# Forward transform moved ahead of the loop, gradient through a padded scratch, last 64 rows of D row-tiled

## Chip, cores, metric

One core of one Trainium2 chip. The metric is device time of the whole program in microseconds (us). Times are medians, and runs of one kernel lie within 0.5%. Profile times count from the span's start; the span is some 2 to 4 us shorter than the device time.

## The reference

Forward and gradients of a gated mix of two branches: a spectral filter (a 2-D real Fourier transform, a product with weights, the inverse) and a GEGLU feed-forward block.

```python
# x, B_x: 1 x 2048 x 576; w_gate, w_up: 576 x 4608; w_down: 4608 x 576; bfloat16
g = sigmoid((x * gate_w).sum(-1))
a = irfft2(rfft2(x) * (w_r + 1j * w_i))
b = (gelu(x @ w_gate) * (x @ w_up)) @ w_down
out = g * a + (1 - g) * b
# plus the gradients of all inputs but B_x for a given grad_out (all weights and A_x)
# x of both branches is A_x
```

## The kernel before

Everything is written as matmuls. The long loop has 18 groups (256 of the 4608 hidden columns each) of 8 steps (256 rows each). A step does the *hidden matmuls* (gate, up, and gradient through w_down), their elementwise work on ACT and DVE, one or two *weight gradient units* of the group before, and some *transform units* (pieces of the Fourier work) out of a list. After the loop come the output projections.

D is 576 = 4 x 128 + 64. The last chunk was taken as rows 448 to 575, with its first 64 rows zeroed on one side:

```python
DCH = [(0, 128), (128, 128), (256, 128), (384, 128), (448, 128)]
...
def load_dOT(t0):                      # gradient, transposed, 32 small loads
    for t in (t0, t0 + 1):
        LD.dma_start_transpose(dOT[:, 0:4, t, :], do_v[:, t, 0:512])
        LD.dma_start_transpose(dOT[:, 4:5, t, :], do_v[:, t, DCH[4][0]:D])
    nc.gpsimd.memset(dOT[0:D4NEW, 4, t0:t0 + 2, :], 0.0)
...
ph = ...tile_pool(name="ph", bufs=4, space=PSUM)   # hidden matmuls, 1 bank each
pw = ...tile_pool(name="pw", bufs=2, space=PSUM)   # weight gradients
pf = ...tile_pool(name="pf", bufs=1, space=PSUM)   # transform units, 2 banks
...
def H_mm(g, tp):
    for w, xt in ((wg_g, xT), (wu_g, xT), (wdT_g, dOT)):
        pt = ph.tile([P, TPB, FG], F32, tag="hps", name="hps")
        for tt in range(TPB):
            for ci in range(5):
                nc.tensor.matmul(pt[:, tt, :], lhsT=xt[:, ci, tp * TPB + tt, :], rhs=w[:, ci, :],
                                 start=(ci == 0), stop=(ci == 4))
...
fft = fx[:4] + at + fx[4:] + fg + mid[:-2] + ...   # fx: x's transform, fg: the gradient's
def want(step, half):                  # how many units by this half step
    h = 2 * step + half
    if h <= 2 * NT:
        n = max(0, h - 4)              # 12 units in group 0
```

PSUM is the memory that matmuls write to, in banks. A transform unit is a few matmuls into `pf` in PSUM, a copy out by ACT (or DVE) to `Y` or `Vt`, and often a store (x's units store `Vt` to `scr_x`). `LD` is the sync engine's (SP's) DMA queue, which issues in program order.

## Time and profile before

| | before |
|---|---|
| device time | 1581.0 us |
| span | 1576.6 us |
| first hidden matmul | 9.5 us |
| group 0 | 73.0 us |
| groups 1 to 15 | 923.9 us, 61.6 each |
| group 16 (no transform units) | 50.0 us |
| first matmul of the output projections | 1130.2 us |

PE (the matrix engine) carries the time: it is at work 96% of the span, and half of its idle time (35 of 66.5 us) lies in the first 160 us. The lines are in the prediction below. Two habits help in reading them. The "mean ns" of a matmul is a latency; the spacing of starts is what a stream costs. And the busy share of a whole run says little about a stage, so the starts of the groups, read from the timeline, are what everything here is measured by.

### The profile page before, as it was taken

To read this page: it belongs to the slowest core of one execution; us is meant where nothing else is said; L and a number is where in the kernel's file an instruction comes from. 1 tells how busy PE (TensorE), PEld (TensorE's weight loads), DVE (VectorE), ACT (ScalarE), POOL (GpSimd) and SP (SyncE) were. 2 spreads that over 40 slices of the span, in tenths; PEclk is the share of its full clock that TensorE was granted. 3 is DMA by queue.
4 is the path that set the end of the run, shared out by engine and by line. 5 is a ranking of instruction groups with operands and counts; after the bars stand their busy time and mean duration, and the time that the engine had idled before them with its cause. 6 is when DMAs were issued, how large, how long until landed. Compare 5 with 4: busy or idle time off the path is not lost.

```text
span 1576.6 us, 33157 instructions
## 1 busy us (share of the span) xinstructions
PE 1510.1 (96%) x13310; PEld 1270.9 (81%) x13310; DVE 813.9 (52%) x2154; ACT 738.8 (47%) x1395; POOL 26.3 (2%) x58
## 2 busy tenths in 40 slices
PE   6798999999999999999999999999997999999998
PEld 4577888888788888888888888888876777777776
DVE  5775565666887877865555646667103212121210
ACT  6777665765766766665666656656000000000000
POOL 1000000000000000000000000000000000000000
PEclk8999999999999999999999999999999999999999
DMA  6632432334544544453424434364899978787873
GB/s 140 198 102 78 113 99 82 109 97 132 140 134 120 151 124 129 132 152 93 124 82 135 127 97 128 101 145 122 241 192 214 212 153 172 155 171 154 170 150 69
DMA packets 513435, 214.45 MB, mean 136 GB/s; under 512 B 318080, under 2 KB 506368, under 8 KB 513280
## 3 DMA queue, kind: packets, MB, share of 16 engines
q1 hardware_dynamic: 511648, 207.61, 54.5%
q0 software_dynamic: 1632, 4.72, 1.1%
q8 instruction: 104, 1.70, 0.5%
q14 instruction: 51, 0.42, 0.1%
HBM read 41.77 MB, written 94.71 MB: 87 GB/s over the span
## 4 chain that ended last, share of the span: by engine, by line
PE 62%; issue 23%; DVE 6%; ACT 6%; DMA 1%; POOL 1%; SPq 1%; POOLq 0%; DVEq 0%; ACTq 0%
PE hps L312 25%; PE wps L392 15%; PE wps L376 7%; PE pf L640 3%; PE acc L833 2%; PE wps L403 2%; PE pf L433 2%; PE acc L875 2%; ACT da L334 1%; ACT om L330 1%; ACT q L323 1%; DMA pin<-scr 1%; PE pf L624 1%; PE pf L626 1%; ACT xb L324 1%
## 5 line engine op out<-in xcount | busy, mean ns | idle before, releaser
L312 PEld LDWEIGHTS <-xT 128*128 128x128 bf16 x2880 | 286.0, 99 | 39.6
L875 PEld LDWEIGHTS <-pin 128*128 128x128 bf16 x2304 | 225.4, 98 | 58.3 <-DMA pin<-scr 1.6
L392 PEld LDWEIGHTS <-xn 128*128 128x128 bf16 x2304 | 223.9, 98 | 30.3 <-issue 3.6
L312 PE MATMUL hps<-wg_g,xT 128*128 128x256 bf16 x1440 | 186.5, 278 | 0.0
L312 PE MATMUL hps<-wu_g,xT 128*128 128x256 bf16 x1440 | 183.8, 275 | 0.0
L312 PE MATMUL hps<-wdT_g,dOT 128*128 128x256 bf16 x1440 | 180.8, 273 | 0.0
L325 DVE TENSOR_SCALAR s<-q 128x512 bf16<-128x512 bf16 x144 | 42.0, 291 | 254.0 <-ACT q L323 253.8
L312 PEld LDWEIGHTS <-dOT 128*128 128x128 bf16 x1440 | 141.0, 98 | 16.4
L833 PE MATMUL acc<-wd_all,pin 128*128 128x288 bf16 x1152 | 145.4, 288 | 8.1 <-DMA pin<-scr 6.6
L376 PE MATMUL wps<-dB,A 128*128 128x288 bf16 x1152 | 152.2, 286 | 0.0
L875 PE MATMUL acc<-wuT,pin 128*128 128x288 bf16 x1152 | 143.4, 286 | 1.3 <-DMA pin<-scr 1.3
L833 PEld LDWEIGHTS <-pin 128*128 128x128 bf16 x1152 | 113.2, 98 | 38.5 <-DMA pin<-scr 7.5
L875 PE MATMUL acc<-wgT,pin 128*128 128x288 bf16 x1152 | 143.4, 286 | 0.0
L376 PEld LDWEIGHTS <-A 128*128 128x128 bf16 x1152 | 112.7, 98 | 27.6
L392 PE MATMUL wps<-dHu,xn 128*128 128x256 bf16 x1152 | 131.7, 273 | 0.0
L392 PE MATMUL wps<-dHg,xn 128*128 128x256 bf16 x1152 | 131.5, 273 | 0.0
L323 ACT ACTIVATE q<-hps 128x512 bf16<-128x512 f32 x144 | 86.1, 598 | 94.9 <-PE hps L312 94.9
L885 ACT COPY f32t<-acc 128x576 f32<-128x576 f32 x16 | 10.2, 638 | 250.5 <-PE acc L875 250.5
L334 ACT ACTIVATE da<-hps,omg 128x256 bf16<-128x256 f32 x288 | 118.1, 460 | 0.0
L887 DVE SCALAR_TENSOR_TENSOR f32t<-gwf,dlog,f32t 128x576 f32<-128x576 f32 x16 | 13.1, 818 | 179.1 <-ACT f32t L885 179.1
L330 ACT ACTIVATE om<-s 128x512 bf16<-128x512 bf16 x144 | 91.0, 632 | 24.5 <-DVE s L326 23.9
L331 ACT ACTIVATE s<-s 128x512 bf16<-128x512 bf16 x144 | 90.7, 630 | 4.6
(164 smaller groups left out, 1760.9 us busy)
## 6 DMA issues: line engine op xcount, KB each, us to landing
scr<-A SPq DMA_DIRECT2D x144, 128.0 KB, 1.9
scr<-dHg SPq DMA_DIRECT2D x144, 128.0 KB, 1.9
scr<-dHu SPq DMA_DIRECT2D x144, 128.0 KB, 1.9
out_dram<-dw SPq DMA_DIRECT2D x72, 128.0 KB, 1.8
out_dram<-dwd SPq DMA_DIRECT2D x36, 144.0 KB, 2.0
wd_all<-in_B_w_down_dram SPq DMA_DIRECT2D x3, 1728.0 KB, 12.6
scr_p<-Vt SPq DMA_DIRECT2D x32, 144.5 KB, 2.3
Vp<-scr_p SPq DMA_DIRECT2D x16, 289.0 KB, 3.4
```

Of the source, the lines that this page charges most:

```text
L312: nc.tensor.matmul(pt[:, tt, :], lhsT=xt[:, ci, tp * TPB + tt, :], rhs=w[:, ci, :], start=(ci == 0), stop=(ci == 4))
L323: nc.scalar.activation(q[:], hg[:], ACT.Square)
L325: V.tensor_scalar(s[:], q[:], A_GELU, 1.0, op0=ALU.mult, op1=ALU.add)
L330: nc.scalar.activation(om[:], s[:], ACT.Sigmoid, scale=-2.0 * C_GELU)
L331: nc.scalar.activation(s[:], s[:], ACT.Sigmoid, scale=2.0 * C_GELU)
L334: nc.scalar.activation(da[:, tt, :], da_ps[:, tt, :], ACT.Copy, scale=omg32[:, t0 + tt:t0 + tt + 1])
L376: nc.tensor.matmul(wps[:, :288], lhsT=tl(0, t)[:, fch * P:(fch + 1) * P], rhs=dB[:, t, h * 288:(h + 1) * 288], start=(t == 0), stop=(t == ...
L392: nc.tensor.matmul(wps[:, cc, :], lhsT=xn[:, t, (c0 + cc) * P:(c0 + cc + 1) * P], rhs=tl(k, t), start=(t == 0), stop=(t == T - 1))
L403: nc.tensor.matmul(wps[r0:r0 + 64, 0, :], lhsT=xn[:, t, 512:576], rhs=tl(k, t), start=(t == 0), stop=(t == T - 1))
L640: nc.tensor.matmul(yps[:, h, :288], lhsT=Z[:, lc, c, :], rhs=tb.At[lc][:, c, h * 288:(h + 1) * 288], start=(n == 0), stop=(n == 5))
L833: nc.tensor.matmul(bps[:, h, :288], lhsT=At[:, r, :], rhs=wd_all[:, fc, h * 288:(h + 1) * 288], start=(fc == 0), stop=(fc == NFC - 1))
L875: nc.tensor.matmul(xps[:, h, :288], lhsT=src[:, r, :], rhs=wT[:, h * 288:(h + 1) * 288], start=(k == 1 and f0 + r == 0), stop=(k == 2 and ...
```

## The change

The intent: (1) give the last 64 rows of D to half of the array's rows, two row tiles at once, so that five matmuls become four and a half; (2) put gate and up side by side in one 512-column matmul; (3) run x's part of the first stage of the transform (all of its 32 units, up to the store to `scr_x`) before the loop, while weights and gradient load; (4) replace 32 small transposing loads of the gradient by a padded copy in DRAM and four large ones; (5) retune the pace of units and the order on ACT. Core of the diff, cut:

```diff
+    for k in range(4):
+        load_x(4 * k)
+    do_s = [dram.tile([4, P, 5 * P], BF16, name=f"do_s{k}") for k in range(4)]
+    for k in range(4):
+        src = do_v[:, 4 * k:4 * k + 4, :].rearrange("p t d -> t p d")
+        LD.dma_start(do_s[k][:, :, 0:D], src)
+        LD.dma_start(do_s[k][:, :, D:], src[:, :, 512:D])
     wts = {0: load_w(0)}
+    for k in range(4):
+        LD.dma_start_transpose(dOT[:, :, 4 * k:4 * k + 4, :].rearrange("d c t p -> d c (t p)"),
+                               do_s[k][:].rearrange("t p d -> (t p) d"))
...
-    ph = ps1.enter_context(tc.tile_pool(name="ph", bufs=4, space=PSUM))
+    ph = ps1.enter_context(tc.tile_pool(name="ph", bufs=1, space=PSUM))   # xy, 2 banks
+    pz = ps1.enter_context(tc.tile_pool(name="pz", bufs=1, space=PSUM))   # z, 2 banks
...
+        if tp % 2 == 0:                               # z for two steps
+            ... 16 full matmuls of 256 columns ...
+            for t in range(t0, t0 + 4):
+                r = (LO, HI)[t % 2]
+                nc.tensor.matmul(zt[0][:, t % 2, (t - t0) // 2, :], lhsT=dOT[r, 4, t, :], rhs=wdT[r, 4, :],
+                                 start=False, stop=t >= t0 + 2)
+        for tt, r in enumerate((LO, HI)):             # xy: gate and up
+            nc.tensor.matmul(xy[:, tt, :], lhsT=xT[r, 4, t0 + tt, :], rhs=wgu[r, 4, :], start=True, stop=False)
+        for tt in range(TPB):
+            for ci in range(4):
+                nc.tensor.matmul(xy[:, tt, :], lhsT=xT[:, ci, t0 + tt, :], rhs=wgu[:, ci, :], ...)
...
+    for t in range(T):                                # the head, before the loop
+        x1[t]()
+        ... transposes of x, tables ...
+        if t > 0:
+            x2[t - 1]()                               # ends in a store through LD
...
-            n = max(0, h - 4)
+            n = max(0, 3 * (h - 1) // 2)              # 22 units in group 0
```

More of the change, by code (lines that the diff above doesn't have):

```diff
@@ L37 @@
 IMM = bass.MemoryType
-def load_w_dchunks(nc, eng, dst, w, fsl):
-    eng.dma_start(dst[:, 0:4, :], w[0:512, fsl].rearrange("(c p) f -> p c f", p=P))
-    eng.dma_start(dst[:, 4, :], w[DCH[4][0]:D, fsl])
+LO, HI = slice(0, 64), slice(64, 128)
 class Unit:
@@ L66, in iotas @@
     G.iota(tb.dcol[:, 0:4], pattern=[[128, 4]], base=0, channel_multiplier=1, **kw)
-    G.iota(tb.dcol[:, 4:5], pattern=[[0, 1]], base=DCH[4][0], channel_multiplier=1, **kw)
+    for r in (LO, HI):
+        G.iota(tb.dcol[r, 4:5], pattern=[[0, 1]], base=512, channel_multiplier=1, **kw)
     tb.krow = res.tile([P, P], F32, name="krow")
@@ L211, in load_w @@
         fsl = slice(g * FG, (g + 1) * FG)
-        wg_g = wpool.tile([P, 5, FG], BF16, tag="wg_g", name="wg_g")
-        wu_g = wpool.tile([P, 5, FG], BF16, tag="wu_g", name="wu_g")
-        wdT_g = wpool.tile([P, 5, FG], BF16, tag="wdT_g", name="wdT_g")
-        load_w_dchunks(nc, LD, wg_g, B_w_gate, fsl)
-        load_w_dchunks(nc, LD, wu_g, B_w_up, fsl)
-        LD.dma_start_transpose(wdT_g[:, 0:4, :], B_w_down[fsl, 0:512])
-        LD.dma_start_transpose(wdT_g[:, 4:5, :], B_w_down[fsl, DCH[4][0]:D])
-        return wg_g, wu_g, wdT_g
+        wgu = wpool.tile([P, 5, 2 * FG], BF16, tag="wgu", name="wgu")
+        wdT = wpool.tile([P, 5, FG], BF16, tag="wdT", name="wdT")
+        for k, w in enumerate((B_w_gate, B_w_up)):
+            cols = slice(k * FG, (k + 1) * FG)
+            LD.dma_start(wgu[:, 0:4, cols], w[0:512, fsl].rearrange("(c p) f -> p c f", p=P))
+            for r in (LO, HI):
+                LD.dma_start(wgu[r, 4, cols], w[512:D, fsl])
+        LD.dma_start_transpose(wdT[:, 4:5, :], B_w_down[fsl, DCH[4][0]:D])
+        LD.dma_start_transpose(wdT[:, 0:4, :], B_w_down[fsl, 0:512])
+        LD.dma_start(wdT[LO, 4, :], wdT[HI, 4, :])
+        return wgu, wdT
     def load_dOT(t):
@@ L223, in load_dOT @@
         LD.dma_start_transpose(dOT[:, 4:5, t, :], do_v[:, t, DCH[4][0]:D])
-    nc.gpsimd.memset(xT[0:D4NEW, 4, :, :], 0.0)
+    nc.gpsimd.memset(gwT[LO, 4:5], 0.0)
     ident = res.tile([P, P], BF16, name="ident")
@@ L230 @@
         nc.gpsimd.dma_start(gwT[:, 0:4], gate_w[0:512].rearrange("(c p) -> p c", p=P))
-        nc.gpsimd.dma_start(gwT[:, 4:5], gate_w[DCH[4][0]:D].rearrange("(p o) -> p o", o=1))
+        nc.gpsimd.dma_start(gwT[HI, 4:5], gate_w[512:D].rearrange("(p o) -> p o", o=1))
     def load_x(t0):
@@ L237, in load_do @@
         LD.dma_start(dB[:, t0:t0 + 4, :], do_v[:, t0:t0 + 4, :])
-    def load_dOT(t0):
-        for t in (t0, t0 + 1):
-            LD.dma_start_transpose(dOT[:, 0:4, t, :], do_v[:, t, 0:512])
-            LD.dma_start_transpose(dOT[:, 4:5, t, :], do_v[:, t, DCH[4][0]:D])
-        nc.gpsimd.memset(dOT[0:D4NEW, 4, t0:t0 + 2, :], 0.0)
-    load_x(0)
+    for k in range(4):
[5 more added lines that the diff above has]
+        LD.dma_start(do_s[k][:, :, D:], src[:, :, 512:D])
     wts = {0: load_w(0)}
-    load_dOT(0)
-    for k in range(1, 4):
-        load_x(4 * k)
-        load_dOT(2 * k)
+    for k in range(4):
+        LD.dma_start_transpose(dOT[:, :, 4 * k:4 * k + 4, :].rearrange("d c t p -> d c (t p)"),
+                               do_s[k][:].rearrange("t p d -> (t p) d"))
     gwb = res.tile([P, D], BF16, name="gwb")
@@ L267, with headps, x_chunk @@
     tb.Rt = []
-    def x_chunk(t0, act):
-        for k, c0 in enumerate((0, 2, 4)):
-            nc_ = min(2, 5 - c0)
-            tp_ = ph.tile([P, 2, 4, P], BF16, tag="hps", name="tp")
-            for c in range(nc_):
-                d0 = DCH[c0 + c][0]
-                for tt in range(4):
-                    nc.tensor.transpose(tp_[:, c, tt, :], xn[:, t0 + tt, d0:d0 + 128], ident[:])
-            p0 = D4NEW if c0 == 4 else 0
-            o, i = xT[p0:, c0:c0 + nc_, t0:t0 + 4, :], tp_[p0:, 0:nc_]
-            if k in act:
+    hctr = [0]
+    def headps():
+        hctr[0] += 1
+        pool, tag = ((pf, "pf"), (ph, "xy"), (pz, "z"))[hctr[0] % 3]
+        return pool, tag
+    def x_chunk(t0):
+        for k, cs in enumerate(((0, 1), (2, 3), (4,))):
+            pool, tag = headps()
+            tp_ = pool.tile([P, 2, 2, 4, P], BF16, tag=tag, name="tp")
+            for j, c in enumerate(cs):
+                for tt in range(4):
+                    if c < 4:
+                        nc.tensor.transpose(tp_[:, 0, j, tt, :], xn[:, t0 + tt, c * P:(c + 1) * P], ident[:])
+                    else:
+                        for r in (LO, HI):
+                            nc.tensor.transpose(tp_[r, 0, 0, tt, :], xn[:, t0 + tt, 512:D], ident[:])
+            o = xT[:, cs[0]:cs[0] + len(cs), t0:t0 + 4, :]
+            i = tp_[:, 0, 0:len(cs)]
+            if k == (t0 // 4) % 2:
                 nc.scalar.copy(o, i)
@@ L282, in x_chunk, with gate @@
                 V.tensor_copy(o, i)
-    def gate(t0):
+    def gate():
         lps = pw.tile([P, 512], F32, tag="wps", name="lps")
-        for t in range(t0, t0 + 4):
+        for t in range(T):
             for ci in range(5):
-                nc.tensor.matmul(lps[:, t - t0:t - t0 + 1], lhsT=xT[:, ci, t, :], rhs=gwT[:, ci:ci + 1],
+                nc.tensor.matmul(lps[:, t:t + 1], lhsT=xT[:, ci, t, :], rhs=gwT[:, ci:ci + 1],
                                  start=(ci == 0), stop=(ci == 4))
-        sl = slice(t0, t0 + 4)
-        nc.scalar.activation(g_bf[:, sl], lps[:, 0:4], ACT.Sigmoid)
-        V.tensor_copy(g32[:, sl], g_bf[:, sl])
-        V.tensor_scalar(omg_bf[:, sl], g32[:, sl], -1.0, 1.0, op0=ALU.mult, op1=ALU.add)
-        V.tensor_copy(omg32[:, sl], omg_bf[:, sl])
@@ L296 @@
-    x_chunk(0, (0, 1, 2))
-    build_D(nc, tb, unit, res)
-    build_R(nc, tb, unit, 0)
-    run_late(tb)
-    gate(0)
+        nc.scalar.activation(g_bf[:], lps[:, 0:T], ACT.Sigmoid)
+        V.tensor_copy(g32[:], g_bf[:])
+        V.tensor_scalar(omg_bf[:], g32[:], -1.0, 1.0, op0=ALU.mult, op1=ALU.add)
+        V.tensor_copy(omg32[:], omg_bf[:])
     kept = {}
+    zt = [None]
     def H_mm(g, tp):
-        wg_g, wu_g, wdT_g = wts[g]
-        out = []
-        for w, xt in ((wg_g, xT), (wu_g, xT), (wdT_g, dOT)):
-            pt = ph.tile([P, TPB, FG], F32, tag="hps", name="hps")
-            for tt in range(TPB):
-                for ci in range(5):
-                    nc.tensor.matmul(pt[:, tt, :], lhsT=xt[:, ci, tp * TPB + tt, :], rhs=w[:, ci, :],
-                                     start=(ci == 0), stop=(ci == 4))
-            out.append(pt)
-        return out
+        wgu, wdT = wts[g]
+        t0 = tp * TPB
+        if tp % 2 == 0:
+            zt[0] = pz.tile([P, 2, 2, FG], F32, tag="z", name="z")
+            for t in range(t0, t0 + 4):
+                for ci in range(4):
+                    nc.tensor.matmul(zt[0][:, t % 2, (t - t0) // 2, :], lhsT=dOT[:, ci, t, :], rhs=wdT[:, ci, :],
+                                     start=(t < t0 + 2 and ci == 0), stop=False)
+            for t in range(t0, t0 + 4):
+                r = (LO, HI)[t % 2]
+                nc.tensor.matmul(zt[0][:, t % 2, (t - t0) // 2, :], lhsT=dOT[r, 4, t, :], rhs=wdT[r, 4, :],
+                                 start=False, stop=t >= t0 + 2)
+        xy = ph.tile([P, 2, 2 * FG], F32, tag="xy", name="xy")
+        for tt, r in enumerate((LO, HI)):
+            nc.tensor.matmul(xy[:, tt, :], lhsT=xT[r, 4, t0 + tt, :], rhs=wgu[r, 4, :], start=True, stop=False)
+        for tt in range(TPB):
+            for ci in range(4):
+                nc.tensor.matmul(xy[:, tt, :], lhsT=xT[:, ci, t0 + tt, :], rhs=wgu[:, ci, :], start=False, stop=(ci == 3))
+        return xy[:, :, 0:FG], xy[:, :, FG:2 * FG], zt[0][:, :, tp % 2, :]
@@ L322, in H_ew1 @@
         xb, q, s, om, hu, da = (ewt(n) for n in ("xb", "q", "s", "om", "hu", "da"))
-        nc.scalar.activation(q[:], hg[:], ACT.Square)
-        nc.scalar.copy(xb[:], hg[:])
+        t0 = tp * TPB
+        for tt in range(TPB):
+            nc.scalar.activation(da[:, tt, :], da_ps[:, tt, :], ACT.Copy, scale=omg32[:, t0 + tt:t0 + tt + 1])
+        nc.scalar.activation(q[:], hg, ACT.Square)
+        nc.scalar.copy(xb[:], hg)
+        nc.scalar.copy(hu[:], hu_ps)
         V.tensor_scalar(s[:], q[:], A_GELU, 1.0, op0=ALU.mult, op1=ALU.add)
@@ L328, in H_ew1, with H_sig @@
         V.tensor_tensor(q[:], xb[:], q[:], op=ALU.mult)
-        nc.scalar.copy(hu[:], hu_ps[:])
+        return xb, q, s, om, hu, da
+    def H_sig(tiles):
+        xb, q, s, om, hu, da = tiles
         nc.scalar.activation(om[:], s[:], ACT.Sigmoid, scale=-2.0 * C_GELU)
         nc.scalar.activation(s[:], s[:], ACT.Sigmoid, scale=2.0 * C_GELU)
-        t0 = tp * TPB
-        for tt in range(TPB):
-            nc.scalar.activation(da[:, tt, :], da_ps[:, tt, :], ACT.Copy, scale=omg32[:, t0 + tt:t0 + tt + 1])
-        return xb, q, s, om, hu, da
     def H_ew2(g, tp, tiles):
@@ L355 @@
     ectr = [0]
+    wst = [LD]
     def wevac(out, in_):
@@ L383, in f @@
                     r0 = g * FG + fch * P
-                    LD.dma_start(out_6[r0:r0 + P, :], dwd[:])
+                    wst[0].dma_start(out_6[r0:r0 + P, :], dwd[:])
             return f
@@ L388, in f @@
             def f():
+                late = k == 2 and c0 + TPB >= 4
                 wps = pw.tile([P, TPB, FG], F32, tag="wps", name="wps")
@@ L394, in f @@
                 dw = stage.tile([P, TPB, FG], BF16, tag="dw", name="dw")
-                wevac(dw[:], wps[:])
-                LD.dma_start(ov[:, c0:c0 + TPB, fsl], dw[:])
+                (nc.scalar.copy if late else wevac)(dw[:], wps[:])
+                wst[0].dma_start(ov[:, c0:c0 + TPB, fsl], dw[:])
             return f
@@ L406, in u_tail @@
             wevac(dw[:], wps[:, 0, :])
-            LD.dma_start(out_4[512:576, fsl], dw[0:64, :])
-            LD.dma_start(out_5[512:576, fsl], dw[64:128, :])
-        us = [u_dw(1, o4v, c0) for c0 in range(0, 4, TPB)]
+            wst[0].dma_start(out_4[512:576, fsl], dw[0:64, :])
+            wst[0].dma_start(out_5[512:576, fsl], dw[64:128, :])
+        dw1, dw2 = ([u_dw(k, ov, c0) for c0 in range(0, 4, TPB)] for k, ov in ((1, o4v), (2, o5v)))
         ud = [u_dwd(fch, h) for fch in range(FCH) for h in range(2)]
-        us = us + ud if g == 0 else ud + us
-        us += [u_tail]
-        us += [u_dw(2, o5v, c0) for c0 in range(0, 4, TPB)]
-        return us
+        if g == 0:
+            return dw1 + ud + [u_tail] + dw2
+        return [ud[0], dw1[0], ud[1], ud[2], ud[3], dw1[1], u_tail] + dw2
     side = []
@@ L423, in pftile, with fwd_units @@
         return pf.tile([P, 2, 512], F32, tag="pf", name="pf")
-    def fwd_units(src, dst, scale):
+    def fwd_units(src, dst, scale, ps=pftile, vevac=None):
         ys = {}
@@ L429, in f @@
             def f():
-                yps = pftile()
+                yps = ps()
                 for c in range(2):
-                    for ci in range(5):
+                    for ci in range(4):
                         nc.tensor.matmul(yps[:, c, :DF], lhsT=src[:, ci, t, :], rhs=tb.Dt[ci][:, c, :],
-                                         start=(ci == 0), stop=(ci == 4))
+                                         start=(ci == 0), stop=False)
+                for c, r in enumerate((LO, HI)):
+                    nc.tensor.matmul(yps[:, c, :DF], lhsT=src[r, 4, t, :], rhs=tb.Dt[4][r, c, :], start=False, stop=True)
                 ys[t] = unit([2, DF], name="Y")
@@ L445, in f @@
                 R = tb.Rt[t]
-                vps = pftile()
+                vps = ps()
                 nc.tensor.matmul(vps[:, 0, :DF], lhsT=R[:, 0, :], rhs=Y[:, 0, :], start=True, stop=False)
@@ L451, in f @@
                 Vt = unit([2, DF], name="Vt")
-                nc.scalar.copy(Vt[:], vps[:, :, :DF])
+                if src is xT or t < 8:
+                    V.tensor_copy(Vt[:], vps[:, :, :DF])
+                else:
+                    nc.scalar.copy(Vt[:], vps[:, :, :DF])
                 LD.dma_start(dst[t], Vt[:])
@@ L463, in f @@
             for c in range(2):
-                for ci, (d0, dn) in enumerate(DCH):
-                    nc.tensor.transpose(tps[:, c, d0:d0 + dn], tb.Dt[ci][:, c, l0:l0 + ln], ident[:])
+                for ci in range(4):
+                    nc.tensor.transpose(tps[:, c, ci * P:(ci + 1) * P], tb.Dt[ci][:, c, l0:l0 + ln], ident[:])
+                nc.tensor.transpose(tps[:, c, 512:D], tb.Dt[4][LO, c, l0:l0 + ln], ident[LO, LO])
             o = unit([2, D], name="At")
@@ L655, in inv_units, with head_tile @@
         return out + [d(T - 1)], [pre(0), pre(2)]
-    fx = zipped(*fwd_units(xT, scr_x, None))
+    def head_tile():
+        pool, tag = headps()
+        return pool.tile([P, 2, 512], F32, tag=tag, name="fx")
+    build_D(nc, tb, unit, res)
+    x_chunk(0)
+    run_late(tb)
+    x1, x2 = fwd_units(xT, scr_x, None, ps=head_tile)
+    build_R(nc, tb, unit, 0)
+    run_late(tb)
+    for t in range(T):
+        x1[t]()
+        if t % 4 == 2 and t < 14:
+            x_chunk(t + 2)
+        if t % 3 == 0 and t + 3 < T:
+            build_R(nc, tb, unit, t + 3)
+            run_late(tb)
+        if t > 0:
+            x2[t - 1]()
+    build_B(nc, tb, unit, res)
+    run_late(tb)
+    gate()
+    x2[T - 1]()
     fg = zipped(*fwd_units(dOT, scr_g, g32))
@@ L662 @@
     mid = mid_units()
-    fft = fx[:4] + at + fx[4:] + fg + mid[:-2] + [load_At] + pa + mid[-2:] + [gap] * 2 + ia[:-4] + pb + ia[-4:] + ib
+    fft = at + fg + [gap] * 3 + mid[:-2] + [load_At] + pa + mid[-2:] + [gap] * 2 + ia[:-4] + pb + ia[-4:] + ib
     fft_pos = [0]
@@ L676 @@
     LAST = NG * NT - 16
+    PACE = [0, 1, 3, 4, 6, 7, 8, 10, 11]
+    slot0 = 3 * (2 * NT - 1) // 2
     done = [0]
@@ L682, in want @@
         if h <= 2 * NT:
-            n = max(0, h - 4)
+            n = max(0, 3 * (h - 1) // 2)
         else:
-            n = 2 * NT - 4 + (n_slots - 2 * NT + 4) * (h - 2 * NT) / (2.0 * (LAST - NT))
+            tp = step % NT
+            n = slot0 + (n_slots - slot0) * ((step - tp - NT) / NT + (PACE[tp] + half * (PACE[tp + 1] - PACE[tp]) / 2) / PACE[NT]) \
+                / ((LAST - NT) / NT)
         return int(min(n, n_slots) + 1e-9)
@@ L700, in load_wgT, with early_loads @@
             wgT_all.extend([u[:, 0], u[:, 1]])
-    def early_x(k):
-        def f():
-            x_chunk(4 * k, (0, 1))
-            gate(4 * k)
-            if k < 3:
-                load_dOT(4 + 4 * k)
-                load_dOT(6 + 4 * k)
-            if k == 3:
-                for t0 in range(0, T, 4):
-                    load_do(t0)
-        return f
-    def early_R(t0):
-        def f():
-            build_R(nc, tb, unit, t0)
-            run_late(tb)
-        return f
-    def early_B():
-        build_B(nc, tb, unit, res)
-        run_late(tb)
-        LD.dma_start(gwb[:], gate_w.partition_broadcast(P))
-    def early_w():
-        wts[1] = load_w(1)
-    early = {0: early_x(1), 1: early_x(2), 2: early_x(3), 3: early_R(3), 4: early_w, 16: early_B}
-    for t0 in range(6, T, 3):
-        early[t0] = early_R(t0)
+    def early_loads():
+        for t0 in range(0, T, 4):
+            load_do(t0)
+        wts[1] = load_w(1)
+        LD.dma_start(gwb[:], gate_w.partition_broadcast(P))
+    early = {1: early_loads}
     wgT_from = 108
     pend = []
-    quota = [0, 1, 1, 1, 2, 1, 2, 1]
+    carry = []
+    quota = [0, 1, 1, 1, 2, 1, 1, 1]
     for g in range(NG):
@@ L740 @@
             fft_until(want(step, 1))
+            H_sig(tiles)
+            if carry:
+                carry.pop()()
             H_ew2(g, tp, tiles)
@@ L756 @@
                     side.pop(0)()
-        assert not pend
+        assert len(pend) <= 1
+        carry = pend
         pend = W_units(g)
@@ L790 @@
         LD.dma_start(wd_all[:, f0:f0 + FCB, :], wd_v[:, f0:f0 + FCB, :])
-    for u in pend:
+    wst[0] = nc.scalar
+    for u in carry + pend:
         u()
```

## The prediction

> **What bounds the kernel now.** I read the page first (busy shares, slices, costliest groups), then a table of stages over time windows, then the timeline of the matrix engine at the starts of the loop's groups, and last single instructions around a change of tile shape. The page:
>
> ```profile
> span 1576.6 us, 33157 instructions
> PE 1510.1 (96%) x13310; PEld 1270.9 (81%) x13310; DVE 813.9 (52%) x2154; ACT 738.8 (47%) x1395; POOL 26.3 (2%) x58
> PE   6798999999999999999999999999997999999998
> L312 PE MATMUL hps<-wg_g,xT 128*128 128x256 bf16 x1440 | 186.5, 278 | 0.0
> L312 PE MATMUL hps<-wu_g,xT 128*128 128x256 bf16 x1440 | 183.8, 275 | 0.0
> L312 PE MATMUL hps<-wdT_g,dOT 128*128 128x256 bf16 x1440 | 180.8, 273 | 0.0
> ```
>
> PE is the bound at 96%; only the first four of the 40 slices and one near 1180 us are less than nine tenths full. The three L312 groups are what the change rewrites: 4320 matmuls, none of which ever waited (idle 0.0). The mean of 278 ns is latency, not spacing: ten of them take 1.25 us with the last one's drain, so one starts every 0.109 us.
>
> The stage table (columns: PE, PEld, DVE, ACT, POOL busy, granted clock, DMA share, GB/s):
>
> ```profile
> 0.00:160.00 160.00, 125.21 (x1128) 104.06 (x1129) 104.61 (x307) 115.64 (x205) 8.49 (x25) 0.95 0.48 129
> 160.00:1106.00 946.00, 930.55 (x8469) 804.50 (x8467) 628.80 (x1681) 599.99 (x1153) 0.00 (x0) 1.00 0.43 119
> 1140.00:1576.60 436.60, 420.33 (x3410) 333.78 (x3407) 77.19 (x161) 20.42 (x32) 17.84 (x33) 0.99 0.85 165
> ```
>
> The idle PE time sits in the first 160 us (35 us of it). From 160 us to the end of the loop, PE is filled, so there a matmul taken out is time saved, and a drain put in is time lost. The last part (output projections) is not touched.
>
> The loop has 18 groups of 8 steps. Their starts in the PE timeline:
>
> ```profile
> 9.51 2.29 PE L312 MATMUL hps<-wg_g,xT 128*128 128x256 bf16 x10
> ...
> 82.50 2.15 PE L312 MATMUL hps<-wg_g,xT 128*128 128x256 bf16 x10
> ...
> 1006.43 1.26 PE L312 MATMUL hps<-wg_g,xT 128*128 128x256 bf16 x10
> ...
> 1056.42 1.25 PE L312 MATMUL hps<-wg_g,xT 128*128 128x256 bf16 x10
> ```
>
> Group 0 begins at 9.5 and takes 73.0 us; groups 1 to 15 take 923.9, or 61.6 each; group 16, which has no transform units, takes 50.0. One group holds 240 hidden matmuls at 0.109 = 26.2, so its weight gradients take 23.8; the 11.6 more in groups 1 to 15 are transform units and waits.
>
> **What the Trainium skill says.** (1) TensorE: Matmul & The Clock Gate, Back-to-back issue gap: a warm matmul of N columns is followed after N/2.4 + 2.5 ns: 109 for 256, 123 for 289, 216 for 512. The trace agrees for the first two; 512 doesn't occur in it. (2) The same page, Part 3 (packing small matmuls): matmuls in different row groups run side by side, starting about 4 ns apart. (3) TensorEngine Tiling (Array Packing), Key Properties: a change of tiling mode drains the engine; its Gotcha 1 adds that different row tiles must write different PSUM banks, and the new code does put the two halves into two banks. The old kernel has only column tiles, but they show both the pairing and the drain:
>
> ```profile
> 498.60 0.29 PE L586 MATMUL pf<-n,Rt 128*128 128x289 bf16 x1
> 498.82 0.30 PE L403 MATMUL wps<-dHg,xn 128*64 128x256 bf16 x1
> 498.82 0.30 PE L403 MATMUL wps<-dHu,xn 128*64 128x256 bf16 x1
> 498.95 0.27 PE L403 MATMUL wps<-dHg,xn 128*64 128x256 bf16 x1
> ...
> 500.48 0.27 PE L403 MATMUL wps<-dHu,xn 128*64 128x256 bf16 x1
> 500.69 3.56 PE L392 MATMUL wps<-dHu,xn 128*128 128x256 bf16 x31
> ```
>
> Pairs start together (498.82 twice). Entering takes 0.22 us where 0.123 is normal, leaving 0.21 where 0.109 is: 0.10 us per switch. (4) DMA: Bandwidth & Descriptors, Anatomy of one DMA: the DMA engines don't wait on semaphores, the issuing sequencer does. All loads and stores here go through SP in order, so one waiting transpose holds every store behind it. In the old trace, stores and transposes do follow one another in SP's one sequence.
>
> **The change, part by part.**
>
> *Hidden matmuls.* Per two steps the old kernel has 60 x 0.109 = 6.56 us. The new one has 16 full ones of 256 columns for z (1.75), 16 full ones of 512 for gate and up together (16 x 0.216 = 3.45), one pair of pairs for z's last 64 rows (0.22) and two pairs of 512 (0.43), 5.85 in all. The order on PE is z full, z rows, xy rows, xy full, xy rows, xy full: four switches, 0.40. Sum 6.25, so 25.0 per group in place of 26.2. More than half of the packing gain of 0.71 goes into drains.
>
> *Transforms.* One unit of the first stage becomes 8 x 0.123 + 0.123 + 0.20 = 1.31 in place of 1.23: no gain, a small loss. All transform work in the loop was: x and gradient 16 x 14 x 0.123 = 27.6 each, table transposes 1.7, the middle 64 x 4 x 0.123 = 31.5, the inverses 32 x (6 x 0.109 + 12 x 0.1225) = 68; sum 156. About 9 of it fell into group 0, so 147/15 = 9.8 in each of groups 1 to 15, and 1.8 of their 11.6 are waits. In the new kernel x's 27.6 leave the loop and 22 slots run in group 0 (about 19 us), so 110/15 = 7.4 stay per group. The buffer for gate and up has no second copy now; after each of its matmul blocks ACT needs about 0.2 + 0.50 + 0.49 + 0.60 = 1.8 us to empty it (spacings in the chain of waits), and PE has at least one gradient unit (1.9 to 3.5 us) or the z block (2.0) in between. I take 1.5 of waits per group. A group is then 25.0 + 23.8 + 7.4 + 1.5 = 57.7, 3.9 less: 15 x 3.9 = 58.5 us saved, and 2 x 1.2 = 2.4 in groups 16 and 17.
>
> *The head.* It gets x's transform (16 x 1.8 = 29 us of PE), the transposes of x and the gate, some 36 us in all, before the first step. Tables are ready at about 13 us as before (the sines ended at 12.4); then a tile costs PE about 2.15 us (1.31 + 0.49 + 0.35 of transposes), DVE about 1.8 and ACT about 1.4, so 16 tiles end near 47. The B table and the gate in line add 3: 50. Beside this SP has to bring in x, copy the gradient to the scratch, load weights, about 6.0 MB before the first large transpose may issue. The window of 60 to 80 us moved 292 GB/s at a DMA share of 0.93, so 21 us, ending near 25. Four transposes of 655 KB follow; six of 393 KB took SP 11.49 us when queues were full, so about 3.2 each, 13 together: near 38. Only then do the stores of x's transform go out, and the instruction order shows buffers waiting on them from about tile 12 (PE there at 39). I add 2 us: first step at 52, 42.5 later than now.
>
> *Group 0.* Now 73.0 us with 40 us of PE work. New: 25.0 of hidden matmuls plus 19 of transforms, 44; DVE has 12 operations per step (4.7 us), copies out of PSUM and the scaling of the gradient, some 48 in all. With start-up, 52: 21.0 less.
>
> *Last groups' stores* move from SP to ACT's queue; PE's first output matmul stood at 1130.20 right behind the last gradient one, so nothing is saved. Sum: +42.5 - 21.0 - 58.5 - 2.4 = -39.4, and 1581.0 becomes 1542.
>
> **Rivals.** *Row pairs don't overlap, or drain longer.* If the two halves ran one after the other, each two steps cost another 0.65 us, 72 x 0.65 = 47: about 1589. If a switch costs 0.2 rather than 0.1, 288 more tenths = 29: about 1571. For it: no row tile is in this trace, and a 512-column matmul may drain longer. Against: column pairs overlap fully here.
>
> *The head becomes a DMA wait.* If DRAM to DRAM copies or the 128-byte tails run at half the rate, the transposes end near 60 and the first step moves to 65 or 70: about 1557. For it: SP's single order. Against: the first-stage work fills most of that time.
>
> *The single buffers bind.* If each step waits 0.4 us for ACT, 144 x 0.4 = 58: 1600 or so. For it: ACT runs in order and holds q, xb and hu until all 16 wide matmuls are done, where before the gate part was free after ten. Against: ACT is 63% busy and the pace list spreads transform slots over the short steps.
>
> *Waits shrink.* If the shifted sigmoid order removes the waits of groups 1 to 15 altogether, 15 x 1.5 = 22: 1520.
>
> **Range and chances.** Two errors of some 12 us (head, switches) and one of 10 (waits) combine to about 18, so 1542, from 1520 to 1565. Faster by over 2% means under 1549.4: 0.64; within 2%: 0.33; slower: 0.03.
>
> **What would show it.** First wide gate-and-up matmul near 52 us; group 0 near 52; groups 1 to 15 near 57.7, groups 16 and 17 near 48.8; row pairs starting within a few hundredths of a us, followed by a full matmul 0.1 us later than the formula; idle 0 in front of the wide row matmuls. Wrong would be: idle there released by ACT, row halves started 0.2 us apart, or a PE gap between 30 and 60 us that ends with a DMA.

## The result

The changed kernel takes 1575.4 us (1572.3 to 1577.8, four runs) against 1581.0: a ratio of 0.9963, interval 0.9945 to 0.9982. Ratios here compare runs of the same rounds, so they are not quite the ratios of the medians quoted. That is the same within 2%. I had predicted 1542, with a range of 1520 to 1565.

In the views, `xy` is gate and up, `z` the gradient through w_down, `dOT` the transposed gradient, `do_s` its padded copy, `fx` the buffers of x's transform; PEclk is the clock granted to PE, in tenths of the full one. From the page of the changed kernel:

```profile
span 1570.5 us, 30102 instructions
PE 1482.8 (94%) x11762; PEld 1080.0 (69%) x11886; DVE 823.7 (52%) x2168; ACT 708.8 (45%) x1357; POOL 22.5 (1%) x51
PE   7377999899999999999999999999998999999998
PEclk9689999999999999999999999999999999999999
L330 PE MATMUL xy<-wgu,xT 128*128 128x512 bf16 x1028 | 257.4, 381 | 13.5 <-issue 10.4
```

The second slice of PE (39 to 79 us) is three tenths full, and its clock six tenths. PE is not fuller than before, it is emptier (94%), and the holes are still at the start, now larger. In the L330 group some first records of blocks are missing from the trace (1028 of 1152); its "issue" idle is mostly that.

Starts of groups 0, 1, 16 and 17 and of the output projections in the PE timeline (start us, us, engine, line, operation; in brackets the idle before and what ended it):

```profile
77.89 3.57 PE L319 MATMUL z<-wdT,dOT 128*128 128x256 bf16 x16 [3.22 <-DVE Vt L475]
...
152.27 0.49 PE L319 MATMUL z<-wdT,dOT 128*128 128x256 bf16 x3
...
1000.95 0.82 PE L319 MATMUL z<-wdT,dOT 128*128 128x256 bf16 x6
...
1049.73 0.82 PE L319 MATMUL z<-wdT,dOT 128*128 128x256 bf16 x6
...
1125.80 2.37 PE L912 MATMUL acc<-wgT,pin 128*128 128x288 bf16 x18
```

The ledger by stage, in us. The last column is the best version of the experiments, told further down.

| stage | before | predicted | changed | three repairs |
|---|---|---|---|---|
| first hidden matmul at | 9.5 | 52 | 77.9 | 53.9 |
| group 0 | 73.0 | 52 | 74.4 | 58.7 |
| groups 1 to 15 | 923.9 | 865.5 | 848.7 | 847.9 |
| group 16 up to the output projections | 123.8 | 121.4 | 124.8 | 124.8 |
| output projections | 446.4 | 446.4 | 444.7 | 445.5 |
| span | 1576.6 | 1537 | 1570.5 | 1530.8 |

So the loop proper did gain 75 us (3.5 of them are one weight gradient unit that now runs after the loop, in the next row). The head gave 68 back, and group 0, which should have gained 21, gained nothing. Where the head went, in the timeline of SP's queue of the changed kernel (the second number is how long the queue was held by the issue):

```profile
3.75 6.41 SPq L247 DMA_DIRECT2D do_s<-in_grad_out_dram  x1
10.21 5.97 SPq L246 DMA_DIRECT2D do_s<-in_grad_out_dram  x1
...
27.07 5.90 SPq L246 DMA_DIRECT2D do_s<-in_grad_out_dram  x1
...
47.98 12.20 SPq L250 DMA_TRANSPOSE dOT<-do_s  x4
60.28 5.97 SPq L478 DMA_DIRECT2D scr_x<-Vt  x12
```

and in the PE timeline, the tile after which it stops:

```profile
44.49 0.30 PE L456 MATMUL fx<-Dt,xT 64*128 64x289 bf16 x2
63.63 0.40 PE L469 MATMUL fx<-Y,Rt 128*128 128x289 bf16 x1 [18.84 <-ACT Y L459]
```

and in the view of waits from 40 to 78 us:

```profile
ACT Y L459 <- DMA scr_x<-Vt: 21.5, 1, 21.5
```

Four copies of 576 KB hold the queue some 6 us each. The transposes issue at 48 instead of the 25 that I had worked out, the stores of x's transform behind them at 60, and PE stands 18.8 us because ACT can't get a buffer for Y: ACT waited 21.5 us for one of those stores to land. When PE goes on, its clock has fallen (0.63 on average from 40 to 78 us).

### The profile page after: what moved, and what is told of

Its sections match the earlier page's. It is cut to its first block, busy times and chain, and to the rows that moved or that the text cites. A ratio compares the mean times of both kernels' runs of the same rounds, so it can differ in the third digit from the quotient of the medians.

```text
span 1570.5 us, 30102 instructions
## 1 busy us (share of the span) xinstructions
PE 1482.8 (94%) x11762; PEld 1080.0 (69%) x11886; DVE 823.7 (52%) x2168; ACT 708.8 (45%) x1357; POOL 22.5 (1%) x51
## 3 DMA queue, kind: packets, MB, share of 16 engines
q10 hardware_dynamic: 1808, 1.02, 0.2%
## 4 chain that ended last, share of the span: by engine, by line
PE 68%; issue 23%; SPq 5%; DVE 1%; ACT 1%; POOL 1%; DMA 1%; POOLq 0%; DVEq 0%; ACTq 0%
PE wps L413 16%; PE xy L330 16%; PE wps L396 9%; PE z L319 8%; PE pf L666 3%; PE acc L870 3%; PE xy L327 2%; PE wps L424 2%; PE acc L912 2%; PE z L323 1%; SPq L246 1%; PE pf L453 1%; SPq L247 1%; SPq L250 1%; PE pf L650 1%
## 5 line engine op out<-in xcount | busy, mean ns | idle before, releaser
L330 PE MATMUL xy<-wgu,xT 128*128 128x512 bf16 x1028 | 257.4, 381 | 13.5 <-issue 10.4
L330 PEld LDWEIGHTS <-xT 128*128 128x128 bf16 x1152 | 101.3, 98 | 143.5 <-issue 42.4
L341 ACT ACTIVATE da<-z,omg 128x256 bf16<-128x256 f32 x288 | 121.0, 473 | 103.6 <-PE z L323 103.6
L342 ACT ACTIVATE q<-xy 128x512 bf16<-128x512 f32 x144 | 86.0, 597 | 148.7 <-PE xy L330 148.7
L319 PE MATMUL z<-wdT,dOT 128*128 128x256 bf16 x1152 | 140.9, 277 | 3.2 <-DVE Vt L475 3.2
L870 PEld LDWEIGHTS <-pin 128*128 128x128 bf16 x1152 | 113.3, 98 | 36.6 <-DMA pin<-scr 4.3
L319 PEld LDWEIGHTS <-dOT 128*128 128x128 bf16 x1152 | 114.0, 99 | 19.7 <-issue 3.8
L344 ACT CAST hu<-xy 128x512 bf16<-128x512 f32 x144 | 86.8, 603 | 0.0
```

The costliest lines, as they stand in the source:

```text
L319: nc.tensor.matmul(zt[0][:, t % 2, (t - t0) // 2, :], lhsT=dOT[:, ci, t, :], rhs=wdT[:, ci, :], start=(t < t0 + 2 and ci == 0), stop=False)
L330: nc.tensor.matmul(xy[:, tt, :], lhsT=xT[:, ci, t0 + tt, :], rhs=wgu[:, ci, :], start=False, stop=(ci == 3))
L341: nc.scalar.activation(da[:, tt, :], da_ps[:, tt, :], ACT.Copy, scale=omg32[:, t0 + tt:t0 + tt + 1])
L342: nc.scalar.activation(q[:], hg, ACT.Square)
L344: nc.scalar.copy(hu[:], hu_ps)
L870: nc.tensor.matmul(bps[:, h, :288], lhsT=At[:, r, :], rhs=wd_all[:, fc, h * 288:(h + 1) * 288], start=(fc == 0), stop=(fc == NFC - 1))
```

## The experiments

Two things need a cause, the head (+26 us on the prediction) and group 0 (+22). For the head there were two theories: the copies run on few DMA engines, or x's stores are stuck in SP's order whatever the copies do; and a rival, that a copy from DRAM to DRAM is slow in itself. For group 0: one buffer for the transform units, or else the work of DVE and ACT and the low clock. Besides, row tiling was to be measured by itself. Each kernel is the changed one with the edit shown, and all gave correct results.

### Scratch copies with rows first (e1_spray)

```diff
-        src = do_v[:, 4 * k:4 * k + 4, :].rearrange("p t d -> t p d")
-        LD.dma_start(do_s[k][:, :, 0:D], src)
-        LD.dma_start(do_s[k][:, :, D:], src[:, :, 512:D])
+        src = do_v[:, 4 * k:4 * k + 4, :]
+        dst_ = do_s[k][:].rearrange("t p d -> p t d")
+        LD.dma_start(dst_[:, :, 0:D], src)
+        LD.dma_start(dst_[:, :, D:], src[:, :, 512:D])
```

> Only the order of the dimensions in the eight scratch copies changes (rows first, 128 of them, instead of tiles first, 4); same bytes, same place in the queue. Theory (the copy is spread over 4 of 16 DMA engines because its slowest dimension is 4, which is why a 576 KB copy keeps the sync queue 6 us): the copies take under 2.5 us each, the first large transpose issues near 25 us instead of 48, the first z matmul stands at 50 to 55 us instead of 77.9, time about 1575 - 24 = 1551. Rival (a copy from DRAM to DRAM is slow however it is spread): the first z matmul stays beyond 72 us and the time within 5 us of 1575.

Measured: 1560.4 us, ratio to before 0.9878. The queue's timeline:

```profile
7.67 2.92 SPq L247 DMA_DIRECT2D do_s<-in_grad_out_dram  x1
10.63 1.39 SPq L248 DMA_DIRECT2D do_s<-in_grad_out_dram  x1
12.06 0.78 SPq L247 DMA_DIRECT2D do_s<-in_grad_out_dram  x1
12.89 1.06 SPq L248 DMA_DIRECT2D do_s<-in_grad_out_dram  x1
...
23.43 13.06 SPq L251 DMA_TRANSPOSE dOT<-do_s  x4
```

The copies are out at 14 us instead of 35, the transposes issue at 23.4 (I had predicted 25 for the changed kernel). The same bytes between the same places, so DRAM to DRAM isn't slow in itself. The first z stands at 61.5 and not at 50 to 55: x's stores still go out behind the transposes at 36.6, and PE still waits 6.5 us for a buffer. Part of the gain is lost again: group 0 takes 78.9 us here, 4.5 more than in the changed kernel. PE's waits for the units' buffer in it are the same 15.6 us; but PE is at work 58.2 us instead of 53.0, at a mean granted clock of 0.82 instead of 0.89.

### Eight tiles per copy (g1_outer8)

Is it the number of engines, or the order of addresses?

```diff
-    do_s = [dram.tile([4, P, 5 * P], ...) for k in range(4)]
-        src = do_v[:, 4 * k:4 * k + 4, :].rearrange("p t d -> t p d")
+    do_s = [dram.tile([8, P, 5 * P], ...) for k in range(2)]
+        src = do_v[:, 8 * k:8 * k + 8, :].rearrange("p t d -> t p d")
```

> The scratch copies in two halves of eight tiles instead of four of four, tiles still first, so their slowest dimension is 8; all else as in the changed kernel. Theory (the slowest dimension sets the number of DMA engines, 4 before, 8 now): the rate doubles, the copies, which held the sync queue until 35 us, are done near 20, the DMA share in that stretch rises from 0.28 to about 0.5, the large transposes issue near 33 us and the first z matmul stands between the 77.9 of 4 and the 61.5 of 16 engines, near 67; time about 1565. Rival (rows first helps by the order of addresses, not by the number of engines): share stays near 0.28, first z beyond 75, time 1575.

Measured: 1558.2 us, ratio 0.9866, first z at 63.7. The table of windows while the copies run (the columns after each engine's busy time are granted clock, DMA share and GB/s), for the changed kernel with slowest dimension 4:

```profile
12.00:33.00 21.00, 20.02 (x167) 12.96 (x167) 12.44 (x32) 13.59 (x23) 0.00 (x0) 1.00 0.28 81
```

with slowest dimension 8:

```profile
8.00:18.00 10.00, 7.73 (x57) 4.38 (x56) 7.10 (x21) 7.25 (x15) 0.00 (x0) 1.00 0.55 159
```

and with rows first, 128, in the run e1_spray:

```profile
5.00:14.00 9.00, 6.46 (x44) 3.81 (x42) 8.63 (x25) 6.11 (x11) 0.00 (x0) 1.00 1.02 328
```

The share of the 16 engines goes 0.28, 0.55, 1.02 and the rate 81, 159, 328 GB/s: 4, 8 and 16 engines at about 20 GB/s each. The windows are not quite alike: the third still has x's loads in its first 3.5 us. From 10 to 14 us only the copies run in all three, with shares 0.27, 0.54 and 1.13 and 96, 191 and 346 GB/s, so 22 to 24 per engine. The order of addresses with 8 is the same as with 4, so it is the number. (The engines are not listed in these views; their number is read from the shares and the rates. A share above 1 only means that the times of packets overlap.) The Trainium skill has the rule, in DMA: Bandwidth & Descriptors, Why a DMA increments its semaphore by 16 and not by 1: the number of engines is the largest up to 16 that divides the slowest dimension of both sides. I had read that page for the wait on semaphores and not for this.

### x's stores on ACT's queue (e2_act_stores)

```diff
-                LD.dma_start(dst[t], Vt[:])
+                (nc.scalar if src is xT else LD).dma_start(dst[t], Vt[:])
```

> Only the 16 stores of x's transform go out on the scalar engine's queue instead of the sync queue. Theory (the 18.8 us PE gap is the one sync queue: buffers wait for stores that stand behind the transposes): the gap at 45 to 63 us goes, the first z matmul comes when the first transposed chunk lands, about 48 + 4 = 52 to 57 us, time about 1575 - 22 = 1553. Rival (the gap is the DMA engines being full, whichever queue issues): first z matmul beyond 70 us, time within 6 us of 1575.

Measured: 1580.6 us, ratio 1.0006, first z at 83.0. The numbers are those of the rival, but not for its reason. What SP's queue waited for in this kernel, in the view of waits:

```profile
SPq L247 <- DMA scr_x<-Vt: 35.2, 2, 34.1
```

A scratch copy waited 34.1 us for a store of x's transform, which is far behind it in the program. The trace shows why: the program has eight completion semaphores for these DMAs and reuses them in turn. With two queues sharing them the first tail copy was given one (number 116) that two of the stores use, those issued at 16.6 and 35.8 us; it went out at 37.8. The edit took away one wait and made another; as a test it is void.

### x's stores on GpSimd's queue (f1_pool_stores)

The same edit with `ST` (GpSimd, whose DMA semaphores are its own) for `nc.scalar`.

> The stores of x's transform on GpSimd's queue, whose completion semaphores are its own, as the clean form of the run on ACT's queue (there a scratch copy came to wait for a later store). Theory (x's stores stand behind four transposes in the one sync queue): the 18.8 us PE gap before the fourteenth tile goes, then the gradient's first transposed chunk decides: issued at 48 us, landed near 53, so the first z matmul at 52 to 57 us in place of 77.9, time about 1575 - 22 = 1553. Rival (the slow copies alone set the head, moving stores changes nothing): first z beyond 72, time within 5 us of 1575.

Measured: 1558.1 us, ratio 0.9868. PE's 18.8 us gap is gone, and the first z is now held by the gradient:

```profile
60.54 3.59 PE L319 MATMUL z<-wdT,dOT 128*128 128x256 bf16 x16 [9.13 <-DMA dOT<-do_s]
```

60.5, some us later than expected, since here the transposes issue only at 53.9. So both theories of the head hold: taking away the slow copies alone gains 16.4 us (77.9 to 61.5), taking away the queue's order alone 17.4, but the two overlap, as the run with both will show.

### A second buffer for transform units in group 0 (e4_psum2)

The two banks of the weight gradients are idle until group 1.

```diff
+    pgs = ExitStack()
+    pg = [pgs.enter_context(tc.tile_pool(name="pg", bufs=1, space=PSUM))]
...
     def pftile():
+        gct[0] += 1
+        if pg and gct[0] % 2:
+            return pg[0].tile([P, 2, 512], F32, tag="pg", name="pg")
         return pf.tile([P, 2, 512], F32, tag="pf", name="pf")
...
+        if g == 1:                       # give the banks to the weight gradients
+            pg.clear(); pgs.close()
+            pwh.append(ps1.enter_context(tc.tile_pool(name="pw", bufs=2, space=PSUM)))
```

> In group 0 alone the two banks that the weight gradients use from group 1 on serve as a second buffer for transform units. Theory (22 transform units in group 0 take turns in one buffer, each waiting for ACT or DVE to empty it): group 0 falls from 74.4 us to about 56, time about 1575 - 18 = 1557. Rival (group 0 is bound by DVE and ACT work or by the lowered clock): group 0 stays at 70 or more, time within 5 us of 1575.

Measured: 1555.4 us, ratio 0.9844. The head is as before (first z at 78.4); group 0 takes 59.2 us instead of 74.4, where the theory had said about 56 and the rival 70 or more. PE's waits during group 0 in the changed kernel (in total, times, longest):

```profile
PE pf L453 <- DVE Vt L475: 9.9, 6, 2.5
PE pf L469 <- ACT Y L461: 5.7, 6, 1.1
```

and with two buffers:

```profile
PE pg L476 <- DVE Vt L482: 2.5, 2, 1.2
PE pf L460 <- ACT Y L468: 1.4, 3, 0.5
PE pf L476 <- ACT Y L468: 0.8, 1, 0.8
```

15.6 us of waits for the one buffer to be emptied fall to 4.7, which is 11 of the 15 us. Most of the other 4 go with the clock, 1.00 instead of 0.89 between 100 and 120 us: PE is at work 50.2 us in group 0 instead of 53.0. That the fewer waits brought the clock back is likely, but not shown; the run e1_spray has the same waits as the changed kernel and a lower clock, so the waits alone don't set it.

### Row tiling taken out (e3_norow)

In the hidden matmuls the last chunk goes as full 128-row matmuls, with the lower half of the weights zeroed.

```diff
-            for r in (LO, HI):
-                LD.dma_start(wgu[r, 4, cols], w[512:D, fsl])
+            LD.dma_start(wgu[HI, 4, cols], w[512:D, fsl])
+        nc.gpsimd.memset(wgu[LO, 4, :], 0.0)
...
-        for tt, r in enumerate((LO, HI)):
+        for tt, r in enumerate((slice(0, 128), slice(0, 128))):
```

(and the same for z.)

> In the hidden matmuls the last 64 rows of D go as full 128-row matmuls again, the lower half of the weights set to zero; the rest as in the changed kernel. Theory (packing saves 0.65 us per two steps and its four switches cost 0.40): slower by 72 x 0.25 = 18 us, 1593. Rival a (switches eat all): within 5 us of 1575. Rival b (switches cost half of what I took): slower by 72 x 0.45 = 32 us, 1607.

Measured: 1587.7 us, ratio 1.0047, so 12 to 13 us slower than the changed kernel (by the medians, or by the two ratios). Group 16 takes 49.8 instead of 48.8 and groups 4 to 15 about 0.9 more each, which is near the 0.25 per two steps expected; the sum would be 17 to 18 us, but group 3 came out 3 us shorter here, and the two kernels were timed in different rounds. The drains of the changed kernel themselves, in its PE timeline:

```profile
522.87 1.91 PE L319 MATMUL z<-wdT,dOT 128*128 128x256 bf16 x16
524.72 0.39 PE L323 MATMUL z<-wdT,dOT 64*128 64x256 bf16 x4
524.95 0.38 PE L327 MATMUL xy<-wgu,xT 64*128 64x512 bf16 x2
```

and in its timeline of weight loads:

```profile
525.25 1.41 PEld L330 LDWEIGHTS <-xT 128*128 128x128 bf16 x8 [0.32 <-issue]
```

The sixteen full matmuls start 0.109 apart, the last at 524.51, and the row tiles 0.21 later, so entering the row mode costs 0.10. The two 512-column row matmuls together take 0.38 us, the latency of one, so they run side by side. The next full matmul's weights load 0.30 us after their start; 0.216 is the stream time of one, so leaving the row mode costs 0.09 (the matmul's own record is missing; worked back from the next one, at 525.48, it would be 0.11).

### All three repairs (f3_spray_pool_psum2)

The edits of e1_spray, f1_pool_stores and e4_psum2 together.

> All three repairs: scratch copies over 16 DMA engines, x's stores on GpSimd's queue, a second buffer for transform units in group 0. Theory (each removes a wait of its own): first z matmul at 47 to 51 us, the PE work of the head, group 0 at 55 to 58 us, so 1575 - 28 - 18 = 1529, which is what my prediction's terms would have given with the measured 56.6 us in groups 1 to 15. Rival (the waits overlap, the gains don't add): 1540 or more.

Measured: 1532.9 us (1530.7 to 1534.4), ratio 0.9711, interval 0.9696 to 0.9725. This beats both kernels by over 2%. The first z:

```profile
53.90 2.51 PE L322 MATMUL z<-wdT,dOT 128*128 128x256 bf16 x11 [3.48 <-DVE Vt L483]
```

The gains of the head don't add (16.4 and 17.4 alone, 24.0 together), that of group 0 does. 53.9 and 58.7 stand where the prediction had 52 and 52. PE has done the head's work by then, and the remaining 3.5 us are a wait for the last tile's buffer, not for a load.

### x's transform back in the loop (f4_f3_fxloop)

```diff
-    x1, x2 = fwd_units(xT, scr_x, None, ps=head_tile)     # and their calls in the head
+    fx = zipped(*fwd_units(xT, scr_x, None))
-    fft = at + fg + [gap] * 3 + ...
+    fft = fx[:4] + at + fx[4:] + fg + [gap] * 3 + ...
```

on top of the three repairs.

> The three repairs, and x's transform put back into the loop, as before the change; the head keeps the transposes of x, the tables and the gate. Theory (with the head repaired, doing x's transform there pays only for as long as the loads would hold PE anyway): first z near 32 us instead of 49, 17 us earlier, and 28 us more PE work in the loop, so 11 us slower than the three repairs, about 1540. Rival (the head is bound by loads and tables either way): 25 us slower, 1555.

Measured: 1555.3 us, ratio 0.9852: 22 us slower than the repairs alone, near the rival's number, for another reason. The first z stands at 28.8, 25 us earlier, so loads don't hold the head to 50 us (the last 3.4 us before 28.8 are a wait for the gradient's transpose). But groups 1 to 15 take 895.2 instead of 847.9. The 32 units that moved there are about 29 us of PE (16 x 1.31 + 16 x 0.49); the other 18 are not matmul time. PE's waits in groups 1 to 15 say what they are. For ACT or DVE to empty the units' one buffer `pf` PE waits 18.3 us here, in 16 waits, and not at all with the repairs alone. Two of the lines:

```profile
PE pf L461 <- DVE Vt L483: 2.6, 4, 1.2
PE pf L674 <- ACT ZT L663: 2.6, 2, 1.7
```

By the trace it is a single buffer once more, though no run tests it. That the pace list, made for fewer units, brings these waits is only argued. Moving x's transform ahead does pay once the head is not blocked, but most of what it pays in this loop is waits that it avoids there; with a second buffer in the whole loop it might be little, which no run shows.

### The old pace in group 0 (f5_f3_slow0)

```diff
-            n = max(0, 3 * (h - 1) // 2)
+            n = max(0, h - 4)
-    slot0 = 3 * (2 * NT - 1) // 2
+    slot0 = 2 * NT - 4
```

on top of the three repairs.

> The three repairs, and 12 transform units in group 0 instead of 22, the old pace. Theory (with two buffers group 0 is bound by DVE and ACT, some 48 us, and PE has room for the 22): group 0 falls by 8 us or less, the other groups get 10 units of 0.8 us more, so within 4 us of the three repairs. Rival (each unit in group 0 still costs 2 us of waits): group 0 falls by 20 us and the time by 12.

Measured: 1535.8 us, ratio 0.9728, 2.9 us slower than the repairs with 22 units. Group 0 falls to 48.9, by 9.8 us (I had said 8 or less); the later groups take that and more. With two buffers a unit in group 0 costs about 1 us, about what it costs PE, and not the 2 of the rival. The pace of group 0 matters little now (2.9 us).

## Why the prediction was wrong

**The hidden matmuls: right.** 25.0 us per group were predicted, from pairs that overlap and 0.10 per switch. Group 16 was predicted at 48.8 and took 48.8; taking the row tiles out costs 0.9 to 1.0 per group, as the terms had it. (Of the "packing gain of 0.71" per two steps, 0.65 is packing; the rest comes from the wider matmuls.) The rival "row pairs don't overlap, or drain longer" is out.

**Groups 1 to 15: right, a little low in gain.** 57.7 predicted, 56.6 measured. Of the 17 us more, 3.5 are the weight gradient unit that left these groups; most of the rest is fewer waits than the 1.5 per group that I had taken: PE's waits in these groups are 3.8 us for a load and 1.7 for ACT (and 8.7 where records are missing), 0.4 per group. The rival of the single buffers is out: the row matmuls waited for ACT 2.5 us in the whole run.

**The head: wrong.** The step that failed is "The window of 60 to 80 us moved 292 GB/s at a DMA share of 0.93, so 21 us, ending near 25". It took a rate from loads spread over all 16 DMA engines and gave it to copies whose slowest dimension is 4. They ran at 81 GB/s; first transpose at 48. With the copies spread, it issues at 23.4. The rest of that paragraph, stores held behind the transposes and buffers waiting from about tile 12 on, came true, and turned 2 us into 18.8. My rival "the head becomes a DMA wait" named the kind and the place, but with 65 to 70 us and 1557 it was too small, and I had set against it that "the first-stage work fills most of that time", which could not be so once the buffers ran out.

**Group 0: wrong.** "DVE has 12 operations per step ... some 48 in all. With start-up, 52" is the largest of three engines' work. What it left out is that 22 units take turns in one PSUM buffer, each unit's matmuls waiting for the copy of the one before, which stands in the order of ACT or DVE behind the step's own work. Measured 74.4; with two buffers 59.2. The 44 us of PE work also took the full clock for granted; PE was at work 53.0 us there, at a mean granted clock of 0.89. I had thought of buffers only for the hidden matmuls, where the change made them scarcer, and not for the units, where the buffer was as before but the pace was doubled.

**The repairs close the sum.** With both causes taken away the kernel runs at 1532.9, which is 9 us better than predicted: +1.9 in the head, +6.7 in group 0, -17.6 in groups 1 to 15, +3.4 and -0.9 after them, in all -6.5 of span, and the rest is the smaller difference between span and time. Of group 0's 6.7 us above 52, PE's work is most: 49.2 us at a mean granted clock of 0.92, where I had 44 at the full one. Why the clock stays below full there is open. A slip without consequence: errors of 12, 12 and 10 us combine to about 20, not 18; the range allowed 22.

## What to carry to other kernels

Before a DMA's time is worked out from a rate, look at its slowest dimension on both sides: it decides how many engines carry it, and putting the 128 rows first cost nothing here and gave three and a half to four times the rate. Work moved ahead of a loop is only hidden if its results can leave: ask which queue its stores stand in, and behind what. And when the pace of small units is raised, count the buffers they take turns in, not only the engines' work.

## What the Trainium skill lacked or had wrong

- DMA: Bandwidth & Descriptors has the rule for the number of engines, and these runs agree with it (shares 0.28, 0.55, 1.02 for slowest dimensions 4, 8, 128). Its "~27 GiB/s" per engine (Specifications) was not reached by copies from DRAM to DRAM with rows of 1152 bytes: about 20 GB/s each with the 128-byte tails, 24 at best (96 GB/s on 4).
- The same page doesn't say how long such a copy holds the issuing queue: 6 us for the DMAs issued behind 576 KB on 4 engines, 0.7 to 2.9 us on 16.
- TensorEngine Tiling (Array Packing), Key Properties, says that a mode switch drains, but not what it costs: 0.09 to 0.11 us per switch here, for column tiles and row tiles alike, more than half of what packing the last 64 rows saved. It doesn't weigh the two against each other.
- TensorE: Matmul & The Clock Gate, Back-to-back issue gap: its N/2.4 + 2.5 ns, which it calls the gap of an isolated matmul, held in a stream with a weight load before each for the 512-column matmuls that the kernel before did not have (eight of them start to finish of stream in 1.73 us, from 523.08 to 524.81 in the run without row tiles, 0.216 each). Its sustained figure for such a stream, 131 ns at 512 columns, was not seen.
- No page read here mentions that completion semaphores shared in turn by two queues can make an early DMA wait for a late one: 34.1 us in the run with stores on ACT's queue. That is the doing of the program's scheduler, not of the chip.
